# An attention and two-layer MLP kernel: opening in units of 128 queries, with another order of the first weights

## The chip, the cores and the metric

The kernel runs on one core of one Trainium2 chip. The metric is device time in microseconds (us) of one execution. TensorE is called PE, its weight loads PEld, VectorE DVE, ScalarE ACT, GpSimd POOL, SyncE SP.

## What is computed

Attention over chunks of 32 queries, each against 8 memory tokens and its own chunk with 16 tokens to the left and 8 to the right, then two MLPs. There are 4 x 768 = 3072 tokens, 8 heads of 64. The weights and the coefficients a, b arrive as float64; the rest is fp32.

```python
for c in range(nc):                                  # per chunk of 32 queries
    k_full = np.concatenate([mem_k, k[:, :, l_start:r_end]], axis=2)
    v_full = np.concatenate([mem_v, v[:, :, l_start:r_end]], axis=2)
    scores = scale * np.matmul(q_c, k_full.transpose(0, 1, 3, 2))
    a = np.exp(scores - np.max(scores, axis=-1, keepdims=True))
    out[:, :, c_start:c_end] = np.matmul(a / (np.sum(a, axis=-1, keepdims=True) + 1e-09), v_full)
...
h = x @ w_in;   x = np.maximum(0.01 * h, h) @ w_out     # 512 -> 2048 -> 512
...
h = x @ w_in2                                           # 512 -> 2048 -> 512
P = a[0] + a[1]*h + a[2]*h*h + a[3]*h*h*h
Q = 1.0 + np.abs(b[0])*np.abs(h) + np.abs(b[1])*h*h
out = (P / (Q + 1e-06)) @ w_out2
```

## The kernel before

Tokens are worked off in 6 tiles of 512 per layer. Every large matrix product is three products of numbers split in a rounded high part and a low part (high x high, high x low, low x high). A block `emit_h(c)` (L744 on) is 12 products of 128x512 that make 128 hidden features of a tile; `leaky(c)` (L757 on) makes the activation's high part `g` and a copy `s` on ACT and the low part by one subtraction (L766); `emit_y(c)` is the 12 products back to 512 features. There are 16 hidden blocks per tile.

The **opening** (L869 to L950) makes the attention of the first tile. Its 512 queries are 8 blocks of 64, taken two at a time as 4 units. The order of the instructions is written out by hand, and each engine runs its list in that order:

- `att_q` turns a unit's queries on PE (4 transposes, L368) and ACT scales them into `qT` (L370). `att_k` turns one block's keys (L378) and ACT copies them into `kT` or `kT2` (L380); for the first block the memory keys too (L384).
- `att_b1` is one block's scores, 16 products of 64x32 by 64 into a bank `pss` (L460), where four successive products write four different quarters of the array. DVE takes the maximum (L469) and adds its negative (L472), per block on 128x256 numbers. `unit_e` is ACT's exponential of a unit (L412, 128x512); `unit_n` is sum, 1e-9, reciprocal and product (L418 to L421).
- `unit_t` transposes a unit's probabilities (L428), and ACT copies them with four copies of 64x256 (L433) into a block-diagonal tile (`pall`, `pmore`, `pall2`), whose other quarters POOL has set to zero (L876, L877, L881, L882).
- `unit_x` multiplies with the values (16 products of 128x64 by 64 per block pair, L444), ACT rounds to the high part `xh` (L447) and DVE makes the low part `xl` (L448).
- `heat(n)` issues n idle products of 128x128 into a bank `hot` of its own (L867), which nothing reads.

Then comes the **weights' stage** (L978 to L1008): the float64 weights are turned into fp32 in pairs of 128x512 halves, ONE and TWO. `pair_scale` (L170, ACT) scales the high words, `pair_join` is three operations on DVE (L177, L178, L180), `pair_hi` rounds on ACT (L188), `pair_lo` subtracts on DVE (L194). `emit_h(0)`, (1) and (2) are written between them. Pair 0 holds the first layer's input halves 0 and 1, pair 1 input 2 and output 0, pair 2 input 3 and output 1, pair 3 input 4 and output 2, so that `emit_h(4)` needs the high part of pair 3. The order there is

```python
        emit_h(0)
        pair_scale(0, TWO_)
        pair_scale(1, ONE_)
        run(pair_join(0, TWO_))
        pair_hi(0, TWO_)
        run(pair_join(1, ONE_))
        pair_lo(0, TWO_)
        steps = leaky(0)
```

and `steps`, the subtraction of L766, is run later, after the next join. From L1010 a loop goes over all (tile, hidden block) items, with the attention of later tiles put between them by a table of slots. Loads go out on SP's queue in program order: keys and queries, one half of pair 0, values, the other weights.

Of the kernel before, what the change touches and what calls it, by code (L numbers as in the profile page):

```python
# [9 lines left out]
F32 = mybir.dt.float32  # L10
# [14 lines left out]
def kernel(  # L25
# [166 lines left out]
    def pair_lo(n, hs=BOTH):  # L192
        if n < FC:
            nc.vector.tensor_tensor(out=both(n, 1, hs), in0=sums(n, hs).rearrange("p (h m) -> p h m", m=DM),  # L194
                                    in1=both(n, 0, hs).bitcast(F32),
                                    op=ALU.subtract)
# [105 lines left out]
    room = [t[:, n] for t in early for n in range(4)]  # L302
    rooms = {"k": kb + room[0:6], "v": vb + room[6:12], "q": room[12:16]}
# [15 lines left out]
    def load_q(j):  # L319
        bi, blk = divmod(j, BPS)  # L320
        t = rooms["q"][j // 2] if j < FIRST else raw.tile([P, H, D], F32, tag="qr", name="qr", bufs=1)
        nc.sync.dma_start(out=t, in_=q[bi, :, blk * QB:blk * QB + P, :].rearrange("h p d -> p h d"))
        qr[j] = t
# [49 lines left out]
    def att_k(j):  # L373
# [6 lines left out]
        nc.scalar.copy(out=keys(j)[:, :, NM:NM + CTX], in_=pv[:, :, :CTX])  # L380
        if j % BPS == 0:
            for t in (kT, kT2) if j == 0 else (kT,):
                ends = t.rearrange("p c (g m) -> p c g m", m=NM)[:, :, 0:KW // NM:KW // NM - 1, :]
                nc.scalar.copy(out=ends, in_=pv[:, :, KLOAD:].unsqueeze(2).to_broadcast([P, NP, 2, NM]))  # L384
# [6 lines left out]
    opm = {}  # L391
    pall2 = raw.tile([P, 2, NP, 2, 2, CHUNK], F32, tag="wr", name="pb2", bufs=3)
    mall2 = raw.tile([P, 2, NP, WIN], F32, tag="wr", name="pm2", bufs=3)
    kT2 = raw.tile([P, NP, KW], F32, tag="wr", name="kT2", bufs=3)
    pbs = (pall, pmore[:, 0], pmore[:, 1], pall2)

    def keys(j):
        return kT2 if j < FIRST and j % 2 else kT

    def opb(j):  # L400
        return pbs[j // 2]

    def unit_p(j):
        opm[j] = mall2 if j // 2 % 2 else mall
        return opm[j][:, j % 2]

    def span_of(js):
        return slice(js[0] % 2, js[-1] % 2 + 1)

    def unit_e(js):  # L410
        t = opm[js[0]][:, span_of(js)]
        nc.scalar.activation(out=t, in_=t, func=AF.Exp)  # L412

    def unit_n(js):
        t = opm[js[0]][:, span_of(js)].rearrange("p b c m -> p (b c) m")
        n = NP * len(js)
# [6 lines left out]
    def unit_t(js):  # L423
        t = opm[js[0]][:, span_of(js)].rearrange("p b (i h) m -> p (b i) (h m)", h=2)
        n = NP // 2 * len(js)
        ps = psa.tile([P, 512], F32, tag="acc", name="pst")[:, :n * P]
        for i in range(n):
            nc.tensor.transpose(ps[:, i * P:(i + 1) * P], t[:, i, :], ident)  # L428
        pv = ps.rearrange("p (i e c m) -> p i e c m", i=n, e=2, c=2)
        ov = opb(js[0])[:, span_of(js)].rearrange("p b (i h) e c m -> p (b i) h e c m", h=2)  # L430
# [4 lines left out]
    def unit_x(js):  # L435
        n = len(js) * QB
        ps = psa.tile([P, 512], F32, tag="acc", name="psx")[:, :NP * n]
        xv = ps.rearrange("p (c m) -> p c m", c=NP)
        for b, j in enumerate(js):
            vt = rooms["v"][place("v", j)]  # L440
            pt = opb(j)[:, j % 2].rearrange("p n e c m -> p n e (c m)")
            for p in range(NP):
                for e in range(2):
# [425 lines left out]
    with tc.manual_schedule():  # L869
# [15 lines left out]
        for j in range(FIRST):  # L885
            load_qk(j)
# [206 lines left out]
```

## Time and profile before

| | us |
|---|---|
| runs shown | 1149.51, 1150.01, 1151.37 |
| median | 1150.01 |
| profiled execution | 1148.0 |
| its span | 1146.2 |
| PE busy | 1131.7 (99%) |
| DVE busy | 769.7 (67%) |
| ACT busy | 631.8 (55%) |
| POOL busy | 232.1 (20%) |

The span is what the profile covers of the execution; 1.8 us lie around it. A busy share is an average over the span. The profile's first slice of 28.7 us shows PE at 7 tenths, and the slices after it at 9 or more, until the last. Which engine sets the time in a stage is read from the waits there, not from these shares.

### The profile page before, as it was taken

What the parts mean: (1) busy time and instruction counts of PE and PEld (TensorE: products, weight loads), DVE (VectorE), ACT (ScalarE), POOL (GpSimd) and SP (SyncE); (2) the same over time, 40 slices, a digit from 0 to 9 for tenths busy, and PEclk for the clock granted to TensorE, in tenths of its full rate; (3) what the DMA queues carried; (4) which work ended last, traced back from release to release, by engine and by line L of the source; (5) the groups of instructions that cost most, each with busy time, mean ns of one, the idle gap of its engine ahead of it and who ended that gap; (6) DMA issues with size and microseconds to landing.
All of it is one profiled execution on the core that took longest, in us unless ns stands there. A gap on an engine that the chain in (4) does not pass through costs nothing.

```text
span 1146.2 us, 19651 instructions
## 1 busy us (share of the span) xinstructions
PE 1131.7 (99%) x7616; PEld 928.3 (81%) x7616; DVE 769.7 (67%) x1318; ACT 631.8 (55%) x1149; POOL 232.1 (20%) x264
## 2 busy tenths in 40 slices
PE   7999999999999999999999999999999999999998
PEld 6777788888888888888888888888888888888886
DVE  5887846555565555542345886887887888788775
ACT  4677632232232223223346876776777777777765
POOL 3000302231221322210000222222222222222222
PEclk9999999999999999999999999999999999999999
DMA  9966687797778777742342101001100100100101
GB/s 187 260 178 196 187 226 206 213 251 206 202 215 241 208 196 230 207 142 98 97 133 83 65 1 47 28 1 39 36 1 29 46 1 15 59 1 1 37 1 37
DMA packets 148472, 131.98 MB, mean 115 GB/s; under 512 B 63296, under 2 KB 118944, under 8 KB 148380
## 3 DMA queue, kind: packets, MB, share of 16 engines
q1 hardware_dynamic: 143372, 123.25, 37.6%
q0 software_dynamic: 4864, 7.45, 2.8%
q8 instruction: 60, 0.98, 0.4%
q14 instruction: 32, 0.26, 0.1%
q10 hardware_dynamic: 144, 0.03, 0.0%
HBM read 92.92 MB, written 37.75 MB: 114 GB/s over the span
## 4 chain that ended last, share of the span: by engine, by line
PE 95%; DVE 3%; ACT 1%; issue 1%; POOL 0%; DVEq 0%; POOLq 0%
PE hps L753 45%; PE acc L849 23%; PE acc L811 22%; PE psx L667 2%; PE pss L625 1%; PE pss L460 1%; PE hot L867 1%; DVE wwall L178 1%; PE psx L444 0%; PE psx L514 0%; DVE wwall L180 0%; PE psk L378 0%; DVE wwall L177 0%; ACT w L188 0%; DVE w L194 0%
## 5 line engine op out<-in xcount | busy, mean ns | idle before, releaser
L811 PE MATMUL acc<-g,w 128*128 128x512 f32 x1152 | 278.7, 391 | 0.1
L849 PE MATMUL acc<-w,g 128*128 128x512 f32 x1152 | 275.4, 389 | 0.0
L849 PEld LDWEIGHTS acc<-w,g 128*128 128x128 f32 x1152 | 216.2, 188 | 44.8
L811 PEld LDWEIGHTS acc<-g,w 128*128 128x128 f32 x1152 | 214.7, 188 | 46.1 <-ACT w L188 0.5
L763 ACT ACTIVATE g<-hps 128x512 fp32r<-128x512 f32 x96 | 57.4, 598 | 307.1 <-PE hps L753 307.1
L789 POOL TENSOR_TENSOR g<-R,g 128x512 fp32r<-128x512 f32 x96 | 124.2, 1294 | 504.4 <-ACT g L788 466.1
L753 PE MATMUL hps<-xh,w 128*128 128x512 f32 x768 | 209.0, 395 | 3.8 <-ACT pm L484 1.5
L753 PE MATMUL hps<-yh,w 128*128 128x512 f32 x768 | 204.1, 389 | 0.0
L766 DVE TENSOR_TENSOR g<-s,g 128x512 fp32r<-128x512 f32 x96 | 66.2, 690 | 177.6 <-ACT s L764 174.4
L753 PEld LDWEIGHTS hps<-xh,w 128*128 128x128 f32 x768 | 141.2, 188 | 34.6 <-ACT w L188 2.0
L753 PEld LDWEIGHTS hps<-yh,w 128*128 128x128 f32 x768 | 144.3, 188 | 29.9
L590 POOL DMA_DIRECT2D vb<-in_v_dram x128 | 83.2, 651 | 260.5 <-PE psx L667 207.9
L776 ACT ACTIVATE A<-hps 128x512 f32<-128x512 f32 x96 | 57.2, 596 | 113.9 <-PE hps L753 113.9
L792 DVE SCALAR_TENSOR_TENSOR A<-A,small,pb 128x512 f32<-128x512 f32 x96 | 72.0, 750 | 56.2 <-ACT pb L777 56.2
L753 PE MATMUL hps<-xl,w 128*128 128x512 f32 x384 | 103.0, 390 | 0.0
L753 PE MATMUL hps<-yl,w 128*128 128x512 f32 x384 | 102.6, 389 | 0.0
L783 DVE SCALAR_TENSOR_TENSOR A<-A,pb 128x512 f32<-128x512 f32 x96 | 66.5, 692 | 30.2 <-ACT pb L796 30.2
L753 PEld LDWEIGHTS hps<-xl,w 128*128 128x128 f32 x384 | 72.1, 188 | 15.7
L753 PEld LDWEIGHTS hps<-yl,w 128*128 128x128 f32 x384 | 72.1, 188 | 14.9
L778 ACT ACTIVATE R<-hps,small 128x512 f32<-128x512 f32 x96 | 75.0, 781 | 0.0
L785 DVE SCALAR_TENSOR_TENSOR R<-R,small,A 128x512 f32<-128x512 f32 x96 | 72.2, 752 | 3.4
L794 DVE SCALAR_TENSOR_TENSOR R<-R,small,hps 128x512 f32<-128x512 f32 x96 | 71.8, 748 | 3.4
(112 smaller groups left out, 1140.1 us busy)
## 6 DMA issues: line engine op xcount, KB each, us to landing
wr<-in_moe_w_in_dram SPq DMA_DIRECT2D x32, 512.0 KB
wr<-in_moe_w_out_dram SPq DMA_DIRECT2D x32, 512.0 KB
park_dram<-pb SPq DMA_DIRECT2D x16, 512.0 KB
pb<-park_dram SPq DMA_DIRECT2D x64, 128.0 KB
w_dram<-wwall SPq DMA_DIRECT2D x32, 256.0 KB
wb<-w_dram SPq DMA_DIRECT2D x32, 256.0 KB
kb<-in_k_dram SPq DMA_DIRECT2D x59, 112.0 KB
vb<-in_v_dram POOLq DMA_DIRECT2D x118, 56.0 KB, 3.3
```

The source lines that it names most:

```text
L590: nc.gpsimd.dma_start(out=vw[r + at:r + at + n, c], in_=v[bi, hs, lo:lo + n, :].rearrange("h p d -> p h d"))
L753: nc.tensor.matmul(ps[:, :n], w_[:, ws], x_[:, kk, :], start=(kk == 0 and m == 0), stop=(kk == KC - 1 and m == 2))
L763: nc.scalar.activation(out=gh, in_=ps, func=AF.Prelu, alpha=0.01)
L766: return [lambda: nc.vector.tensor_tensor(out=gl, in0=s, in1=gh.bitcast(F32), op=ALU.subtract)]
L778: nc.scalar.activation(out=R, in_=ps, func=AF.Identity, scale=ncf[:, 3:4], bias=ncf[:, 2:3])
L783: nc.vector.scalar_tensor_tensor(out=A0, in0=A0, scalar=ONE, in1=U0, op0=ALU.add, op1=ALU.mult)
L785: nc.vector.scalar_tensor_tensor(out=R0, in0=R0, scalar=ncf[:, 0:1], in1=A0, op0=ALU.add, op1=ALU.mult)
L789: nc.gpsimd.tensor_tensor(out=gl, in0=R0, in1=gh.bitcast(F32), op=ALU.subtract)
L792: nc.vector.scalar_tensor_tensor(out=A, in0=A, scalar=babs[:, 1:2], in1=U, op0=ALU.mult, op1=ALU.add)
L794: nc.vector.scalar_tensor_tensor(out=R, in0=R, scalar=ncf[:, 1:2], in1=ps, op0=ALU.add, op1=ALU.mult)
L811: nc.tensor.matmul(acc[i][d][:, :n], w_[:, ws], g_, start=(f == 0 and m == 0), stop=(f == FC - 1 and m == 2))
L849: nc.tensor.matmul(acc[i][s], g_[:, ss], w_, start=(f == 0 and m == 0), stop=(f == FC - 1 and m == 2))
```

## The change

The opening's unit becomes 128 queries throughout. A unit's scores stand in one bank (`unit_s`, two halves b), with one maximum and one addition of 128x512 (`unit_m`). Its keys come in two pieces (`unit_ka`, 104 or 88 rows; `unit_kb`, 64 rows), and the key tiles are four, two per unit in turn; POOL copies the memory keys into the second two. Successive products of `unit_s` go in pairs to the same quarter of the array. The probabilities are transposed as before but copied with one copy of 128x512; `unit_x` is 32 products of 64x64 by 32 columns into two banks, with two roundings and two low parts of 128x256 per unit. The four POOL memsets go; one of `pall` comes after the opening. The first `heat` has 12 products; idle products write into banks already read. In the weights' stage `pair_lo(0, TWO_)` stands right behind its `pair_hi`, `pair_scale(1, ONE_)` behind that, and four subtractions (the low parts of `leaky(0)`, (1), (2) and of pair 1's second half) are POOL's. The loads go out unit by unit, a unit's queries and then its two key pieces, followed by the values and weights in turn.

```diff
-    def pair_lo(n, hs=BOTH):
+    def pair_lo(n, hs=BOTH, eng=nc.vector):
...
+    kTs = [kT, kT2, kT34[:, 0], kT34[:, 1]]
+    banks = [psw.tile([P, 512], F32, tag="ps", name="hot")]
+    def heat(n, t=None):
+        t = banks[max(len(banks) - 3, 0)] if t is None else t
+        for _ in range(n):
+            nc.tensor.matmul(t[:, :P], ident, ident, start=True, stop=True)
...
+    def unit_ka(u):
+        ps = turned(kroom[u][:, 0], KROWS if u == 0 else CTX, "psk")
+        a, b = kTs[2 * (u % 2)], kTs[2 * (u % 2) + 1]
+        def upper():
+            nc.scalar.copy(out=a[:, :, NM:NM + CTX], in_=ps[:, :, :CTX])
+            if u == 0:
+                for t in (a, b):
+                    nc.scalar.copy(out=ends(t), in_=ps[:, :, KLOAD:].unsqueeze(2).to_broadcast([P, NP, 2, NM]))
+            nc.scalar.copy(out=b[:, :, NM:NM + CTX - KF], in_=ps[:, :, KF:CTX])
...
+    def unit_s(u, b):
+        for p in range(NP):
+            for e in range(2):
+                r = slice(e * 64, e * 64 + 64)
+                for c in range(2):
+                    o = e * 64 + (p % 2) * CHUNK
+                    at = b * QB + c * CHUNK
+                    nc.tensor.matmul(ps[o:o + CHUNK, b, p // 2, c, :], qt[r, p, at:at + CHUNK],
+                                     kt[r, p, c * KOFF:c * KOFF + WIN], start=True, stop=True)
+    def unit_m(u):
+        nc.vector.tensor_reduce(out=mx, in_=ps, op=ALU.max, axis=AX.X, negate=True)
+        nc.vector.tensor_tensor(out=opm[u].rearrange("p (n m) -> p n m", m=WIN), in0=ps,
+                                in1=mx.to_broadcast([P, 2 * NP, WIN]), op=ALU.add)
...
-        for h in range(2):
-            for c in range(2):
-                nc.scalar.copy(out=ov[c * SB:c * SB + SB, :, h, :, c, :], in_=pv[h * SB:h * SB + SB, :, :, c, :])
+        return (lambda: nc.scalar.copy(out=opt[u], in_=ps)), ps
...
+    def unit_x(u, make):
+        for b in range(2):
+            for p in range(NP):
+                for c in range(2):
+                    for e in range(2):
+                        nc.tensor.matmul(ps[c][e * 64:e * 64 + 64, p, b, :], vt[r, 2 * p + e, :],
+                                         pt[r, b, p // 2, e, p % 2, :], start=True, stop=True)
...
-    def leaky(c):
+    def leaky(c, eng=nc.vector):
...
-        heat(6)
+        heat(12)
...
+        for t in (2, 3):
+            nc.gpsimd.tensor_copy(out=ends(kTs[t]), in_=ends(kT))
...
         emit_h(0)
         pair_scale(0, TWO_)
-        pair_scale(1, ONE_)
         run(pair_join(0, TWO_))
         pair_hi(0, TWO_)
+        pair_scale(1, ONE_)
+        pair_lo(0, TWO_)
         run(pair_join(1, ONE_))
-        pair_lo(0, TWO_)
-        steps = leaky(0)
+        run(leaky(0, nc.gpsimd))
         pair_hi(1, ONE_)
         pair_scale(1, TWO_)
         pair_lo(1, ONE_)
         emit_h(1)
         run(pair_join(1, TWO_))
-        run(steps)
-        steps = leaky(1)
         pair_hi(1, TWO_)
         pair_scale(2, ONE_)
-        pair_lo(1, TWO_)
+        pair_lo(1, TWO_, nc.gpsimd)
+        run(leaky(1, nc.gpsimd))
         emit_h(2)
         run(pair_join(2, ONE_))
-        run(steps)
-        steps = leaky(2)
+        run(leaky(2, nc.gpsimd))
```

**First place: DVE, two units of the opening.** `mx` is the maximum, `pm` (and `pm_105`, `pm_104`, `pb`) the tile of probabilities, `sm` the sums. Before:

```order
L469 TENSOR_REDUCE mx<-pss 128x4
L472 TENSOR_TENSOR pm_105<-pss,mx 128x256
L469 TENSOR_REDUCE mx<-pss 128x4
L472 TENSOR_TENSOR pm_105<-pss,mx 128x256
L418 TENSOR_REDUCE sm<-pm 128x8
L419 TENSOR_SCALAR sm<-sm 128x8
L420 RECIPROCAL sm<-sm 128x8
L421 TENSOR_TENSOR pm<-pm,sm 128x512
L469 TENSOR_REDUCE mx<-pss 128x4
L472 TENSOR_TENSOR pm<-pss,mx 128x256
L469 TENSOR_REDUCE mx<-pss 128x4
L472 TENSOR_TENSOR pm<-pss,mx 128x256
```

and now, from the first unit on:

```order
L472 TENSOR_REDUCE mx<-pss 128x8
L473 TENSOR_TENSOR pm<-pss,mx 128x512
L483 TENSOR_REDUCE sm<-pm 128x8
L484 TENSOR_SCALAR sm<-sm 128x8
L485 RECIPROCAL sm<-sm 128x8
L486 TENSOR_TENSOR pm<-pm,sm 128x512
L472 TENSOR_REDUCE mx<-pss 128x8
L473 TENSOR_TENSOR pm_104<-pss,mx 128x512
```

Two maxima and two additions of a unit have become one of each, over twice the columns, and the first unit's sums now stand ahead of the second unit's maximum.

**Second place: PE, from one unit's keys to the next.** `psk` and `psq` are turned keys and queries, `pss` scores, `pst` turned probabilities, `hot` the idle products. Before:

```order
L867 MATMUL hot<-ident 128x128 x2
L368 MATMUL psq<-ident,early 128x128 x4
L378 MATMUL psk<-ident,early 128x88 x8
L867 MATMUL hot<-ident 128x128
L428 MATMUL pst<-ident,pm 128x128 x4
L460 MATMUL pss<-kT,qT 32x64 x16
L460 MATMUL pss<-kT_106,qT 32x64 x16
```

and now:

```order
L427 MATMUL psk<-ident,early 128x64 x4
L463 MATMUL pss<-kT,qT 32x64 x16
L407 MATMUL psq<-ident 128x128 x2
L427 MATMUL psq<-ident,early 128x128 x4
L427 MATMUL psk<-ident,early 128x64 x4
L427 MATMUL psk<-ident,early 128x88 x4
L463 MATMUL pss<-kT_105,qT 32x64 x16
L407 MATMUL psq<-ident 128x128 x2
L491 MATMUL pst<-ident,pm 128x128 x4
L463 MATMUL pss<-kT_106,qT 32x64 x32
```

The transposes of a unit's probabilities stood between the next unit's keys and scores; they now stand behind the scores of two further units.

**Third place: DVE in the weights' stage,** from the second half of pair 0 on. `wwall` is the joined weights (three operations per half), `w` the low part (L194), `g` the activation's low part. Before:

```order
L177 TENSOR_SCALAR wwall<-wwall 128x512
L178 SCALAR_TENSOR_TENSOR wwall<-wr_93,wwall 128x512
L180 SCALAR_TENSOR_TENSOR wwall<-wr_93,wwall 128x512
L194 TENSOR_TENSOR w<-wwall,w 128x512 x2
L177 TENSOR_SCALAR wwall<-wwall 128x512
L178 SCALAR_TENSOR_TENSOR wwall<-wr_93,wwall 128x512
L180 SCALAR_TENSOR_TENSOR wwall<-wr_93,wwall 128x512
L766 TENSOR_TENSOR g<-s,g 128x512
L194 TENSOR_TENSOR w<-wwall,w 128x512
```

now:

```order
L194 TENSOR_TENSOR w<-wwall,w 128x512
L177 TENSOR_SCALAR wwall<-wwall 128x512
L178 SCALAR_TENSOR_TENSOR wwall<-wr_93,wwall 128x512
L180 SCALAR_TENSOR_TENSOR wwall<-wr_93,wwall 128x512
L194 TENSOR_TENSOR w<-wwall,w 128x512
L177 TENSOR_SCALAR wwall<-wwall 128x512
L178 SCALAR_TENSOR_TENSOR wwall<-wr_93,wwall 128x512
L180 SCALAR_TENSOR_TENSOR wwall<-wr_93,wwall 128x512
L177 TENSOR_SCALAR wwall<-wwall 128x512
```

and on POOL, around the end of the opening:

```order
L345 COPY early<-early 32x1536
L1046 MEMSET pb 128x1024
L829 TENSOR_TENSOR g<-s,g 128x512
L194 TENSOR_TENSOR w<-wwall,w 128x512
L829 TENSOR_TENSOR g<-s,g 128x512 x2
L652 DMA vb<-in_mem_v_dram 8x4x64
```

On DVE the low part of each half now comes right behind its join, with no subtraction of `g` between; on POOL four subtractions stand behind the memset of `pall` and ahead of the later tiles' loads.

## Rows read from the trace of the kernel before

**Rows 1.** Page, part 4: the chain that ended last, by engine.
```profile
PE 95%; DVE 3%; ACT 1%; issue 1%; POOL 0%; DVEq 0%; POOLq 0%
```

**Rows 2.** Windows: from:to us, length, busy us (x) of PE, PEld, DVE, ACT, POOL, PEclk, DMA, GB/s.
```profile
0.00:34.49 34.49, 27.45 (x512) 24.18 (x512) 19.50 (x48) 18.51 (x43) 11.32 (x16) 1.00 1.02 219
34.49:54.29 19.80, 18.28 (x80) 14.07 (x81) 17.45 (x28) 12.27 (x21) 0.00 (x0) 1.00 0.87 225
54.29:84.00 29.71, 29.70 (x284) 23.30 (x284) 25.85 (x39) 22.60 (x62) 0.00 (x0) 1.00 0.65 191
```

**Rows 3.** Chain in order of time, start of the weights' stage and its end: start, us, what.
```profile
35.04 0.44 DVE wwall L177
...
53.19 1.05 ACT w L188
54.29 1.88 PE hps L753 x7
```

**Rows 4.** Timeline of the opening: start us, us, engine, line, tiles, count, [idle before].
```profile
1.37 2.93 PE L867 MATMUL hot<-ident 128*128 128x128 f32 x12 [1.37 <-POOL ident masks.py:199]
4.09 1.06 PE L368 MATMUL psq<-ident,early 128*128 128x128 f32 x4
6.24 0.45 ACT L380 COPY kT<-psk 128x352 f32<-128x352 f32 x1 [0.46 <-PE psk L378]
7.03 0.71 PE L460 MATMUL pss<-kT,qT 64*32 64x64 f32 x32
8.20 0.43 DVE L469 TENSOR_REDUCE mx<-pss 128x4 f32<-128x256 f32 x1
8.30 0.64 PE L867 MATMUL hot<-ident 128*128 128x128 f32 x4
```

**Rows 5.** Timeline, one unit in the steady part of the opening.
```profile
16.79 1.50 ACT L433 COPY pb<-pst 64x256 f32<-64x256 f32 x4 [0.99 <-PE pst L428]
17.81 0.42 DVE L472 TENSOR_TENSOR pm<-pss,mx 128x256 f32<-128x256 f32 x1
18.15 0.41 DVE L469 TENSOR_REDUCE mx<-pss 128x4 f32<-128x256 f32 x1
18.94 0.68 DVE L418 TENSOR_REDUCE sm<-pm 128x8 f32<-128x512 f32 x1
20.01 0.65 ACT L412 ACTIVATE pm<-pm 128x512 f32<-128x512 f32 x1
20.09 0.69 DVE L421 TENSOR_TENSOR pm<-pm,sm 128x512 f32<-128x512 f32 x1
```

**Rows 6.** Window on DVE's work from its first maximum to its last low part.
```profile
8.20:34.89 26.69, 21.14 (x456) 18.52 (x455) 18.20 (x41) 16.34 (x38) 4.08 (x4) 1.00 1.08 239
```

**Rows 7.** Timeline, one cycle of the weights' stage on DVE.
```profile
40.00 0.42 DVE L177 TENSOR_SCALAR wwall<-wwall 128x512 uint32<-128x512 uint32 x1
41.80 0.68 DVE L766 TENSOR_TENSOR g<-s,g 128x512 fp32r<-128x512 f32 x1
41.92 0.62 ACT L188 CAST w<-wwall 128x512 fp32r<-128x512 f32 x1
42.57 0.69 DVE L194 TENSOR_TENSOR w<-wwall,w 128x512 fp32r<-128x512 f32 x1
43.18 0.42 DVE L177 TENSOR_SCALAR wwall<-wwall 128x512 uint32<-128x512 uint32 x1
```

**Rows 8.** Groups by form, 34 to 54 us: busy, mean ns | idle before.
```profile
L170 ACT ACTIVATE wwall<-wr 128x512 f32<-128x512 f32 x5 | 3.3, 671 | 0.0
```

**Rows 9.** Timeline around a subtraction on POOL in the second layer, DVE and POOL.
```profile
698.56 1.29 POOL L789 TENSOR_TENSOR g<-R,g 128x512 fp32r<-128x512 f32 x1 [4.15 <-ACT g L788]
698.68 0.75 DVE L794 SCALAR_TENSOR_TENSOR R<-R,small,hps 128x512 f32<-128x512 f32 x1
699.85 0.69 DVE L783 SCALAR_TENSOR_TENSOR A<-A,pb 128x512 f32<-128x512 f32 x1 [0.42 <-ACT pb L796]
```

**Rows 10.** Groups by form, 0 to 35 us: score products and their weight loads.
```profile
L460 PEld LDWEIGHTS pss<-kT,qT 64*32 64x32 f32 x256 | 3.9, 108 | 0.9 <-issue 0.3 <-ACT kT L380 0.3 <-ACT kT L384 0.2
```

More of the change, by code (lines that the diff above doesn't have):

```diff
@@ L301 @@
     FIRST = tiles_of[0][0][1] // QB
-    room = [t[:, n] for t in early for n in range(4)]
-    rooms = {"k": kb + room[0:6], "v": vb + room[6:12], "q": room[12:16]}
+    rooms = {"k": kb, "v": vb + [early[1][:, n] for n in (2, 3)] + [early[2][:, n] for n in range(4)]}
     def place(kind, j):
@@ L407, in span_of @@
[L407 to L416, printed above, removed]
+    kT34 = raw.tile([P, 2, NP, KW], F32, tag="wr", name="kT34", bufs=3)
+    kroom = [kall[:, 0:2], early[0][:, 0:2], early[0][:, 2:4], early[1][:, 0:2]]
+    kTs = [kT, kT2, kT34[:, 0], kT34[:, 1]]
@@ new lines, with bank @@
+    half = lambda t, n: t.rearrange("p a b c d e -> p (a b c d e)")[:, n * 512:(n + 1) * 512]
+    opm = [mall.rearrange("p b c m -> p (b c m)"), mall2.rearrange("p b c m -> p (b c m)"),
+           half(pall, 0), half(pall, 1)]
+    opt = [pmore.rearrange("p n a b c d e -> p (n a b c d e)")[:, u * 512:(u + 1) * 512] for u in range(4)]
+    oqT, ops = {}, {}
+    banks = [psw.tile([P, 512], F32, tag="ps", name="hot")]
+    def bank(name):
+        banks.append(psw.tile([P, 512], F32, tag="ps", name=name))
+        return banks[-1]
@@ new lines, in turned, with unit_q @@
+    def turned(t, rows, name):
+        ps = bank(name)[:, :NP * rows].rearrange("p (c m) -> p c m", c=NP)
+        t = t.rearrange("p h d -> p (h d)")
+        for p in range(NP):
+            nc.tensor.transpose(ps[:, p], t[:rows, p * P:(p + 1) * P], ident[:rows, :rows])
+        return ps
+    def unit_q(u):
+        ps = turned(early[3][:, u], P, "psq")
+        o = tmp.tile([P, NP, P], F32, tag="A", name="qT")
+        oqT[u] = o
+        return lambda: nc.scalar.mul(out=o, in_=ps, mul=scale)
@@ L861, with run @@
     ONE_, TWO_ = slice(0, 1), slice(1, 2)
-    hot = psa.tile([P, 512], F32, tag="acc", name="hot")
-    def heat(n):
-        for _ in range(n):
-            nc.tensor.matmul(hot[:, :P], ident, ident, start=True, stop=True)
+    def run(fns):
+        for fn in fns:
+            fn()
     with tc.manual_schedule():
@@ L919 @@
-        heat(2)
-        unit_e(unit[U - 1])
-        unit_t(unit[U - 2])
-        pair_scale(0, ONE_)
-        lower.append(unit_x(unit[0]))
-        heat(2)
-        unit_n(unit[U - 1])
-        unit_t(unit[U - 1])
-        lower.append(unit_x(unit[1]))
-        lower.pop(0)()
-        for fn in pair_join(0, ONE_):
-            fn()
+        unit_s(0, 0)
+        heat(2)
+        up_a1 = unit_ka(1)
+        up_a1()
+        up_q1 = unit_q(1)
+        up_q1()
+        unit_s(0, 1)
+        heat(2)
@@ new lines @@
+        unit_m(0)
+        up_b1 = unit_kb(1)
+        up_b1()
+        unit_e(0)
+        unit_n(0)
+        unit_s(1, 0)
+        heat(2)
+        up_q2 = unit_q(2)
+        up_q2()
+        up_a2 = unit_ka(2)
+        up_a2()
+        unit_s(1, 1)
+        heat(2)
+        unit_m(1)
+        up_b2 = unit_kb(2)
+        up_b2()
+        unit_e(1)
+        unit_n(1)
+        unit_s(2, 0)
+        heat(2)
+        up_q3 = unit_q(3)
+        up_q3()
+        up_b3 = unit_kb(3)
+        up_b3()
+        up_a3 = unit_ka(3)
@@ new lines @@
+        up_a3()
+        unit_s(2, 1)
+        heat(2)
+        unit_m(2)
+        up_t0, spare = unit_t(0)
+        up_t0()
+        unit_e(2)
+        unit_s(3, 0)
+        unit_s(3, 1)
+        heat(2)
+        unit_m(3)
+        up_t1, _ = unit_t(1)
+        up_t1()
+        unit_e(3)
+        unit_n(2)
+        x0 = unit_x(0, bank)
+        x0[0]()
+        heat(2)
+        pair_scale(0, ONE_)
+        x1 = unit_x(1, bank)
+        x1[0]()
+        heat(2, spare)
+        unit_n(3)
+        up_t2, _ = unit_t(2)
@@ L1003 @@
         run(pair_join(2, TWO_))
-        run(steps)
         pair_hi(2, TWO_)
```

184 lines of the change are left out of this document (90 added, 94 removed).

## The prediction

> **What bounds the kernel now.** I read the chain that ended last, then the busy time by stage, then the chain and the timeline of the two stages that the change touches. The chain is 95% PE and 3% DVE [rows 1], so a gain must come from the few stretches where PE isn't the end of it. The windows show where they are [rows 2]: until 34.49 us PE is busy 27.45 of 34.49; in the weights' stage, 34.49 to 54.29, 18.28 of 19.80; from 54.29 on 29.70 of 29.71. So 54.29, the start of `emit_h(4)`, is the point to follow: behind it PE has no gap that could absorb a shift, and a shift of that point goes to the end unless a later stage takes it back. Ahead of it two chains follow one another. In the opening it goes through PE, ACT and DVE a unit at a time. In the weights' stage it is DVE's from 35.04 on, until ACT rounds pair 3 at 53.19 (1.05) and `emit_h(4)` starts [rows 3].
>
> The profiled execution took 1148.0 (span 1146.2 and 1.8 around it), 2.0 under the median of the runs shown, 1150.01. The shifts below are worked out in that execution and subtracted from the median.
>
> **The first scores come later.** Six idle products are 12 records and took 2.93, 0.24 a record; later the same ones take 0.64 for 4, 0.16 each [rows 4], though the PEclk column reads 1.00 for the whole opening [rows 2], which is its 2.4 GHz level. The first `heat` now has 12 products, so 12 records more: +2.9 at the early price, +1.9 at the later one. I take +2.9, since they stand in the same early stretch, and keep the difference of 1.0 for the range. So the queries' transposes start near 1.37 + 2 x 2.93 = 7.2 instead of 4.09. From there to the first scores it took 2.94 (4.09 to 7.03); with transposes at about 0.6 instead of 1.06, and the keys' too, I take 1.9, so the first half's scores start at 9.1 and not 7.03. The maximum used to wait for one half and now waits for both, and on PE two idle products, the next unit's turned keys and turned queries stand between the halves: about 0.5 + 0.4 + 0.5 + 0.6 + 0.5 + 0.2 for DVE's memset, so the first maximum is at 11.9, where it was at 8.20 [rows 4]. That is **+3.7**.
>
> **DVE's opening gets shorter.** From its first maximum to its last low part DVE had 18.20 of work in 26.69 [rows 6]; 8.5 were waits, most of them for the next unit's scores, which stood behind the transposes of the unit before last. Now DVE's list holds, for each of 4 units, a maximum and an addition of 128x512, priced as the sum's row (0.68) and the product's (0.69): 1.4; sum to product again 1.84 (18.94 to 20.78) [rows 5]; one join 1.8 and one low part 0.7, as in the weights' stage [rows 7]; eight low parts of 128x256, at the 0.34 to 0.42 of operations of that width that read PSUM (17.81 to 18.15) [rows 5], 0.37 each. Together 5.5 + 7.4 + 2.5 + 3.0 = 18.4. The scores now come ahead of DVE's need, because the transposes are out of their way, so what is left as waits is the exponential (0.65 [rows 5]) ahead of the sums of the first two units, with handovers 1.4. The last low part ends near 11.9 + 18.4 + 1.4 = 31.7 instead of 34.89: **-3.2**. `emit_h(0)` needs the high parts first and moves with it, to about 31.2.
>
> **What costs nothing here.** Four copies (1.50 a unit [rows 5]) become one, off the path: DVE has other units' work meanwhile. POOL's memsets are waited for by nobody. The value products double in number, on a PE that idles 7 of 34.49 [rows 2]; were the last unit's on the path, it would be some tenths more. The loads are no larger, and the weights' scaling on ACT never waited for one (idle 0.0 [rows 8]). With everything 3.2 earlier the loads come nearer: what is left of that cover I don't know, and at worst it costs as much as the 3.2, the lower end of the gain. Outside of that the SP queue's order puts each weight at its old place behind the values.
>
> **The weights' stage gets longer.** Four subtractions of 0.69 leave DVE, but little of this is gain. Before, the cycle of a half was 3.18 (40.00 to 43.18): join 1.8, the subtraction of `g` at 41.80, low part at 42.57; and the rounding on ACT that the low part waits for ran beside it, 41.92 to 42.54 [rows 7]. Now the low part stands right behind its join, and DVE waits for the rounding: 1.87 + 0.65 + 0.61 (42.57 to 43.18) = 3.13, practically the same. Before, the stage had 18.2 of DVE from 34.89 to 53.13. Now: 5 joins x 1.87 = 9.3, four low parts x 0.61 = 2.4, four waits for a rounding x 0.65 = 2.6, the last join of 128x1024 at 3.2 (49.95 to 53.19 less its handover [rows 3] bounds it). To this comes a new wait: the scaling of pair 2's first half (0.67 [rows 8]) stands on ACT behind the rounding of pair 1's second half (0.62), which waits for the join before; DVE used to do `g` and a low part meanwhile, and now has only the next join: 1.3. The other scalings are met by 0.1 to 0.5, 0.7 in all. Sum 19.5, so the stage is **+1.3** longer, and all four subtractions on POOL come to no one's harm if POOL runs beside DVE: 1.29 each [rows 9], where `emit_y(0)` alone may wait some tenths.
>
> **The sum**: -3.2 + 1.3 = -1.9 at `emit_h(4)`, 52.4 instead of 54.29. 1150.01 - 1.9 = **1148.1**. This case's own ends: with the idle products at 0.16, 1.0 less; with the scores' halves close together 0.8 less; with last products and handovers on the path 1.4 more: 1146.3 to 1149.5. A measurement of this kernel can tell 0.2%, 2.3 us: 1147.7 to 1152.3 counts as no change.
>
> **Rivals.** *The opening does better.* DVE's 1.4 of waits go because the sums find their exponential done, and half of the added idle products (1.2) is at the later price: 1148.1 - 2.6 = 1145.5. For it: the idle products halve in price within the opening [rows 4]. Against: nothing in DVE's list stands between a unit's addition and its own sums for the first two units.
>
> *POOL and DVE get in each other's way.* In the weights' stage DVE's joins and low parts read two tiles in SBUF each, and so do POOL's subtractions. Where POOL subtracts in the second layer, the operation beside it (698.68) has an operand in PSUM, and the next one with both in SBUF starts at 699.85, exactly when POOL's ends [rows 9]; but the row gives ACT as what it waited for, so it can't tell. If such a pair can't overlap, POOL's 1.29 goes into DVE's chain where it comes first: most of two of them in front of a join (1.2 + 1.2), the rest behind it (0.3 + 0.4), +3.0: **1151.1**, slower than before; it decides from the moment at which two of the four start ahead of DVE's join. If the joins' first operation, with one tile, waits too, +4.2: 1152.3.
>
> The Trainium skill, "SBUF — State Buffer", section "Who interferes with whom", says that a DVE instruction with two SBUF inputs and a GpSimd instruction that reads SBUF exclude each other for their whole length, in order of issue. It speaks for this rival against my forecast; the trace of before agrees with it and does not show it.
>
> *The score products get slow.* Pairs of successive products now use the same quarter of the array. A weight load takes 0.108 [rows 10]; if half of each pair's second one shows, a half has 8 x 0.05 = 0.4 more, and with two to all eight halves on DVE's path the end moves by +0.8 to +3.2: 1148.9 to 1151.3. Against: a product is recorded twice already, on the same quarter both times. The Trainium skill, "TensorE: Matmul & The Clock Gate", section "What overlaps and what doesn't", says that a weight load runs beside a product in flight only where their row groups differ; no row here shows it for such a pair.
>
> *The change does nothing at the end*, because a load that was hidden comes last: 1150.0; it is in the no-change part of the cases above.
>
> **How the numbers follow.** Forecast 0.42 (its range lies across the bound: 0.19 faster, 0.23 the same), the better opening 0.19 (faster), POOL against DVE 0.25 (0.13 the same, 0.12 slower with its upper price and the forecast's upper end), slow score products 0.14 (0.06 and 0.08, when added to POOL's). Faster 0.38, same 0.42, slower 0.20. The range reaches from 1145.2, just past the better opening, to 1152.8, past POOL's upper price; what is outside is a tenth on either side.
>
> **What would show it.** First maximum at 11.9; last low part of the opening at 31.7; DVE with hardly a wait longer than 0.7 in between; in the weights' stage a wait of 0.6 ahead of each low part and one of 1.3 ahead of pair 2's first join; `emit_h(4)` at 52.4. Wrong would be: operations of DVE with two SBUF tiles that last well over 0.69 or start at the end of a POOL subtraction; score halves of 0.9; an idle time of ACT's scaling that a load ends; or a shift at 52.4 that is not there at the end.

## The result, and the profile after

The changed kernel takes 1156.62 us in the median (1155.04 to 1157.76, 4 runs) against 1149.76 of the kernel before on the same chip: ratio 1.0056, interval 1.0039 to 1.0074. It is slower by 6.9, where the forecast was 1.9 faster. Its profiled execution took 1156.17, 8.2 more than that of before. Three executions in the study, one each in e2, e5 and e8, ran at a far lower clock and are left out of all figures below; e5's profile was one of them, so no row of e5 is shown.

The windows of the changed kernel by stage, columns as in [rows 2]:

```profile
0.00:37.25 37.25, 29.82 (x641) 26.79 (x641) 18.45 (x41) 15.63 (x38) 9.07 (x15) 0.91 1.01 221
37.25:61.74 24.49, 21.40 (x81) 16.40 (x81) 18.52 (x25) 12.10 (x21) 5.56 (x4) 0.86 0.58 142
61.74:91.45 29.71, 29.71 (x284) 23.29 (x284) 25.79 (x39) 22.66 (x62) 0.00 (x0) 1.00 0.65 193
```

`emit_h(0)` starts at 37.25 where it was at 34.49, and `emit_h(4)` at 61.74 where it was at 54.29: +2.8 from the opening, +4.7 from the weights' stage. From there PE is full again, as before [rows 2], and the shift of 7.45 stays; the profiled pair loses some tenths more in small waits behind 143 us, which were not followed up. PEclk, the granted clock of PE as a share of its 2.4 GHz, is new: 0.91 and 0.86 where it was 1.00.

The timeline of the changed kernel (start us, us, engine, line; in brackets the idle time before and what ended it):

```profile
8.36 0.69 PE L463 MATMUL pss<-kT,qT 64*32 64x64 f32 x32
11.30 0.69 DVE L472 TENSOR_REDUCE mx<-pss 128x8 f32<-128x512 f32 x1
25.70 0.66 PE L507 MATMUL psx<-pmore,early 64*64 64x32 f32 x29 [1.13 <-issue]
30.32 1.41 DVE L517 TENSOR_TENSOR xl<-psx,xh 128x256 fp32r<-128x256 f32 x4
35.20 1.49 PE L507 MATMUL psx<-pmore,early 64*64 64x32 f32 x43 [4.38 <-issue]
36.95 0.76 DVE L517 TENSOR_TENSOR xl<-psx,xh 128x256 fp32r<-128x256 f32 x2 [5.22 <-ACT xh L513]
```

The first maximum comes near its forecast (11.9), and at 31.7, where the last low part was forecast, three of the four units have theirs. But PE stops twice in the value products, for 1.13 and, in the middle of the last unit, for 4.38; the last low part ends at 37.71, not at 31.7. "Issue" means that PE waited for nothing that the profile shows. These lengths are idle time. Counted from the start of the last record ahead of them the stops are 1.35 (24.35 to 25.70) and 4.60 (30.60 to 35.20). The windows around the two, PE alone (length, busy, count, PEclk, DMA share, GB/s):

```profile
24.00:26.00 2.00, 0.87 (x56) 1.00 0.56 118
26.00:28.00 2.00, 2.00 (x34) 0.76 0.96 204
30.00:32.00 2.00, 0.82 (x38) 0.89 1.06 376
32.00:34.00 2.00, 0.00 (x0) 0.96 1.08 389
34.00:36.00 2.00, 0.80 (x32) 0.50 1.05 374
38.00:40.00 2.00, 2.00 (x7) 0.50 1.14 213
```

Behind the first stop and during the second the granted clock falls to its lower level of 1.2 GHz (0.50), the second time through most of `emit_h(0)`. It is not what makes PE stop: the column reads 1.00 from 24 to 26, when the first stop begins. From 30 to 36 us the loads run at 374 to 389 GB/s. In the DMA view of the two us in which PE does nothing, from 32 to 34, one row is of another kind, a queue that carries instructions (packets, MB, share):

```profile
q8 instruction: 1, 0.02, 3.3%
```

In the weights' stage DVE and POOL read:

```profile
43.53 1.36 DVE L194 TENSOR_TENSOR w<-wwall,w 128x512 fp32r<-128x512 f32 x1 [0.69 <-ACT w L188]
47.92 1.04 DVE L177 TENSOR_SCALAR wwall<-wwall 128x512 uint32<-128x512 uint32 x1 [1.25 <-ACT wwall L170]
48.94 2.99 POOL L829 TENSOR_TENSOR g<-s,g 128x512 fp32r<-128x512 f32 x2 [0.26 <-DMA small<-in_moe_a_dram]
49.00 1.79 DVE L178 SCALAR_TENSOR_TENSOR wwall<-wr,wwall 128x512 uint32<-128x512 uint32 x1
50.83 1.65 DVE L180 SCALAR_TENSOR_TENSOR wwall<-wr,wwall 128x512 uint32<-128x512 uint32 x1
```

Before, L177 took 0.42 and L194 0.69 [rows 7], and L178, like L180, 0.69 (groups by form, 34 to 54 us):

```profile
L178 DVE SCALAR_TENSOR_TENSOR wwall<-wr,wwall 128x512 uint32<-128x512 uint32 x5 | 3.5, 692 | 0.2
```

Now one of each takes 1.36 (L194), 1.04 (L177), 1.79 (L178) and 1.65 (L180), together 3.35 more, and POOL's two last subtractions take 2.99 where one took 1.29 [rows 9].

### The profile page after: what moved, and what is told of

The parts are those of the page before. It is cut to its first block, busy times and chain, and to the rows that moved or that the text cites. A ratio compares the mean times of both kernels' runs of the same rounds, so it can differ in the third digit from the quotient of the medians.

```text
span 1154.4 us, 19892 instructions
## 1 busy us (share of the span) xinstructions
PE 1137.8 (99%) x7744; PEld 932.9 (81%) x7744; DVE 769.2 (67%) x1308; ACT 629.1 (54%) x1144; POOL 236.4 (20%) x267
## 3 DMA queue, kind: packets, MB, share of 16 engines
q0 software_dynamic: 4864, 7.45, 2.7%
## 4 chain that ended last, share of the span: by engine, by line
PE 92%; SPq 3%; DMA 2%; DVE 1%; ACT 1%; issue 1%; DVEq 0%
PE hps L816 44%; PE acc L912 23%; PE acc L874 22%; PE psx L730 2%; PE pss L688 1%; SPq L315 1%; SPq L166 1%; DMA kb<-in_k_dram 1%; DMA early<-in_k_dram 1%; DVE wwall L178 0%; PE pss L530 0%; PE psx L577 0%; DMA pb<-park_dram 0%; DVE wwall L180 0%; ACT wwall L170 0%
```

## The experiments

Two theories stand. **Instructions**: PE stops because its instructions arrive in pieces of 256, and the opening uses them up faster than they come. **Exclusion**: DVE and POOL can't work at the same time on operands in SBUF. The rivals are a late load of values or the granted clock for the stops, and the waits for roundings for the stage's length.

| run | kernel | median | before, same chip | ratio (95%) |
|---|---|---|---|---|
| e1 | change, subtractions on DVE | 1153.42 | 1148.91 | 1.0027 (1.0011 to 1.0044) |
| e2 | change, weights' stage of before | 1153.98 | 1148.91 | 1.0038 (1.0025 to 1.0051) |
| e3 | change, weights held by 2 us | 1156.90 | 1148.91 | 1.0059 (1.0039 to 1.0080) |
| e4 | change, 6 idle products first | 1155.98 | 1148.91 | 1.0060 (1.0045 to 1.0075) |
| e5 | before, new weights' stage | 1153.66 | 1148.92 | 1.0042 (1.0025 to 1.0059) |
| e6 | change, weights held longer | 1153.42 | 1148.92 | 1.0038 (1.0023 to 1.0053) |
| e7 | e6, weights' stage of before | 1150.09 | 1148.92 | 1.0007 (0.9998 to 1.0017) |
| e8 | e7, 6 idle products first | 1150.58 | 1148.92 | 1.0013 (1.0003 to 1.0023) |
| e9 | e8, no idle products later | 1146.46 | 1149.02 | 0.9981 (0.9972 to 0.9991) |
| e10 | e7, twice the later idle products | 1151.14 | 1149.02 | 1.0015 (1.0006 to 1.0024) |
| e11 | before, new order, all on DVE | 1152.17 | 1149.02 | 1.0029 (1.0018 to 1.0040) |
| e12 | before, four subtractions on POOL | 1152.09 | 1149.02 | 1.0031 (1.0019 to 1.0043) |
| e13 | e2, idle products as in e9 | 1145.80 | 1148.47 | 0.9977 (0.9968 to 0.9987) |

### Where PE stops: e4

```diff
-        heat(12)
+        heat(6)
```

> The changed kernel with 6 idle products at the start instead of 12, so 24 PE instructions fewer ahead of everything. Theory 'instructions come in pieces of 256': both gaps stand again at the 961st and the 1217th of PE's records, that is 12 products' records later in the program (near the 47th of unit 1's 64 value products' records and the 33rd of unit 3's, where they were the 35th and the 21st). Rival 'a semaphore, the values or a bank': the gaps stay at the 35th and the 21st. Time within 1.5 of 1156.6 by the first, since the transfer decides when the gap ends; by the second up to 2 less, as the first scores come 2.7 earlier.

The windows of PE and PEld that end in each stop, first of the changed kernel, then of e4 (busy us and, in brackets, count):

```profile
0.00:24.50 24.50, 23.13 (x471) 20.79 (x472) 12.28 (x27) 11.30 (x28) 8.12 (x14) 1.00 1.02 174
0.00:32.00 32.00, 28.33 (x597) 25.43 (x597) 18.15 (x40) 14.93 (x35) 9.07 (x15) 0.95 1.01 195
```

```profile
0.00:24.80 24.80, 22.91 (x471) 19.85 (x472) 12.66 (x27) 12.06 (x28) 8.12 (x14) 1.00 0.98 182
0.00:31.00 31.00, 26.59 (x597) 23.15 (x597) 18.24 (x40) 14.95 (x35) 9.08 (x15) 1.00 0.97 199
```

Both kernels stop after 471 and after 597 product records, though e4 has 6 products (12 records) fewer ahead. Counted with weight loads and semaphore instructions, as the trace has them, these are the 961st and the 1217th record of PE. So the place in the program moved, and the timeline of e4 shows by how much (and a short stop ahead, which the changed kernel doesn't have):

```profile
15.92 0.42 PE L463 MATMUL pss<-kT,qT 64*32 64x64 f32 x9 [0.52 <-issue]
...
23.80 1.01 PE L507 MATMUL psx<-pmore,early 64*64 64x32 f32 x47
25.50 0.44 PE L507 MATMUL psx<-pmore,early 64*64 64x32 f32 x17 [0.69 <-issue]
...
27.74 1.71 PE L507 MATMUL psx<-pmore,early 64*64 64x32 f32 x97 [0.28 <-issue]
34.14 1.07 PE L507 MATMUL psx<-pmore,early 64*64 64x32 f32 x31 [4.69 <-issue]
```

Unit 1's value products break off after 47 records (35 in the changed kernel), and the 97 behind 27.74 are unit 2's 64 and 33 of unit 3 (21 before): exactly the 12 records of the expectation. A semaphore on a load or a bank belongs to an instruction and would have stopped the same one. Between the two stops lie 126 products and 125 weight loads, and with the five semaphore instructions of PE in the trace 256 instructions. The short stop of e4, at 15.92, stands 512 of PE's instructions ahead of the first of the two. For the first stop the profile names a load of values as well (1.2 on PEld); e4 shows that it wasn't the load. Nor was it the clock: in e4 it reads 1.00 up to 31.00, and the second stop begins at 29.45. The time moved little, as expected.

The instruction queue says what ends a stop. In the changed kernel its transfers run from 22.80 to 24.16 and from 32.76 to 33.81, and PE goes on at 25.70 and 35.20. So it is at every stop of every kernel here: PE goes on 1.2 to 1.6 after a transfer of that queue has ended. The queue's 61 transfers in the changed kernel, at 256 instructions each, also fit PE's program: 7744 product records, as many weight loads and 223 semaphore instructions. Pace alone doesn't make a stop. From the 449th record to the 705th PE took 4.8 and did not stop, and the next piece had been sent for 1.6 after the 449th. Up to the first stop it took 3.7, and the piece was sent for 2.2 after the 705th; up to the second it took 4.9, and the piece was sent for 7.1 after the 962nd, with which PE had gone on.

### What makes the piece late: e3, e6, e7, e10

e3 holds the weights from pair 1 on behind a one-column memset on DVE (after the first join); e6 and e7 load the second half of pair 0 first and hold the rest until the low part of pair 0's first half; e7 has the weights' stage of before as well. The edit of e6 and e7 in the loads:

```diff
+        pair_load(0, TWO_)
         for j in range(4, FIRST):
             load_v(j)
-        pair_load(0, TWO_)
-        pair_load(1)
...
         pair_lo(0, ONE_)
+        nc.vector.memset(raw_half(1, 0)[:, 0:1], 0)
+        pair_load(1)
```

> The changed kernel with the loads of the weights from pair 1 on held back until the first join is done (a one-column memset of their tile, some 2 us later than now). Theory 'PE waits for its own instructions, whose transfer stands behind the weights': the instruction transfer that came at 32.8 comes before 30, the gap of 4.4 goes, emit_h(0) starts near 33 instead of 37.2, about 1152.5. Rival 'the last values land late for want of descriptors, not of bandwidth': the gap stays above 3, time within 1 of 1156.6.

> The changed kernel with the second half of pair 0 loaded ahead of the last values and all further weights held until the low part of pair 0's first half is done (near 30). Theory 'the transfer of PE's instructions stands behind the weights' transfers': the instruction transfer at 32.8 comes before 29.5, the gap of 4.4 shrinks under 1, emit_h(0) starts near 33 and the time falls by 3 to 5, to about 1152.5. Rival 'that transfer is asked for late, whatever else is moving': it still comes 6 to 7 after the crossing (25.7), the gap stays above 3.

> As e6_hold_more, with the weights' stage in the order of the kernel before, all subtractions on DVE: the opening's gain without the gap and without POOL. If both theories hold: emit_h(0) near 32.5, the stage 19.4 to 20, emit_h(4) near 52.5, some 2 us faster than the kernel before, about 1147.5. If the gap stays: as e2_tail_before, +5 over before.

e3 gained nothing: in its trace the instruction transfer came at 32.6 and the second stop was 3.7. e6 and e7 did empty the queues: the +6.9 of the changed kernel became +4.5 in e6 (their intervals overlap a little), and the +5.1 of e2 became +1.2 in e7, a drop clear of the noise, though not to the 1147.5 that was expected. e7 at its second stop, in windows and timeline:

```profile
28.00:30.00 2.00, 2.00 (x26) 1.67 (x26) 0.38 (x2) 0.94 (x2) 0.18 (x1) 0.50 0.00 1
30.00:32.00 2.00, 1.27 (x78) 1.16 (x73) 1.22 (x4) 1.40 (x4) 0.77 (x1) 0.96 0.03 8
```

```profile
26.10 0.66 PE L507 MATMUL psx<-pmore,early 64*64 64x32 f32 x29 [1.67 <-issue]
...
32.83 0.91 PE L507 MATMUL psx<-pmore,early 64*64 64x32 f32 x43 [1.56 <-issue]
```

The second stop shrank from 4.38 to 1.56. But with 1 GB/s moving between 28 and 30 the transfer still came only at 30.4, more than 4 us after PE had gone on at 26.10. So the weights make the second stop longer, by some 3, and are not its root; both the theory of e6 and its rival held in part. Why the next piece comes so late after this stop even with idle queues is open.

e10 is e7 with more idle products, at ten places:

```diff
-        heat(2)
+        heat(4)
```

> As e7_hold_more_tail_before, with 4 idle products in place of 2 at each later place: 80 PE instructions more. Theory of the instructions: gaps at the 961st and 1217th record again, each as long or longer, and one more boundary (1473) close behind; time 0.5 to 2 over e7 (1150.1). Rival 'gaps come from the clock or from idle PE': more idle products close them, and the time is equal or lower.

```profile
28.54 1.25 PE L507 MATMUL psx<-pmore,early 64*64 64x32 f32 x64 [0.57 <-ACT wwall L170]
...
32.04 2.18 PE L507 MATMUL psx<-pmore,early 64*64 64x32 f32 x128 [0.28 <-issue]
```

What the theory expected of the gaps fell, and what the rival expected of them came: the stop behind the 961st record shrank to 0.57 (1.67 in e7; the row names a wait for ACT, but PE goes on 1.5 after an instruction transfer here too), the one behind the 1217th had gone, and the clock stayed at 1.00. The 256 instructions up to the 961st record now took 4.3 instead of 3.8, and the next piece was sent for 1.2 after PE went on, not 4.3 after; why so early is open. But the rival's reason, the clock, doesn't hold, by e4. And the time didn't fall: `emit_h(0)` came no earlier (34.87, and 34.37 in e7), and `emit_h(4)` at 56.03 against 56.41; the median's rise of 1 comes later, as 1.4 between 136 and 164 us in the trace, and was not followed up. The stops were 2.7 shorter; the 20 more idle products are work for PE too (where 4 records took 0.71, 8 take 1.16, at ten places), and presumably took that back. So a full clock that is bought with idle products gained nothing.

### Fewer instructions: e8, e9, e13

> As e7_hold_more_tail_before with 6 idle products at the start. If the first scores set the opening's end (the prediction's +3.7): up to 2.5 faster than e7, about 1145. If the later pace is set by DVE, loads or PE's instructions: the same as e7 within 0.7.

e8 is within 0.7 of e7: its first maximum is earlier (10.37 against 11.15 in the traces), but its stop behind the 961st record is 2.61, and that takes the gain back. So the first idle products are not what the opening waits for.

> As e7_hold_more_tail_before, with 6 idle products at the start and none later: 104 PE instructions fewer in the opening. Theory 'PE runs out of instructions because the opening has too many per us': the crossings at the 705th and 961st record come later, the gap at the 961st (1.9 in e7) is under 0.5 and the next one under 1; emit_h(0) near 32, about 1147.5 if the clock stays at 1.00. Rival 'the idle products hold the clock': the granted clock falls to 0.5 before 24 us, where it was 1.00 in e7, and the time is 1150 or more.

> As e2_tail_before (loads in the order of the change, weights' stage of the kernel before) with the idle products of e9_lean: 6 at the start and none later. If too many PE instructions per us make the gap and the weights' transfers only lengthen it: the gap at the 961st record stays under 1, the one at the 1217th under 2, and the time is within 1.5 of e9 (1146.5). If the weights' transfers make it: a gap of 3 or more comes back, and the time is near e2's 1154.

```diff
-        heat(12)
+        heat(6)
...
-        heat(2)
```

(the last at all ten places). In e9 and e13 both that is the edit, and both are faster than the kernel before. e13, without the hold, is at 0.9977 (0.9968 to 0.9987); it can't be told from e9 (0.9981), so the hold isn't needed. e13 differs from e2 (1.0038) by 26 idle products alone, which are 104 PE instructions. Its timeline (DVE, then PE) and clock:

```profile
11.07 0.69 DVE L472 TENSOR_REDUCE mx<-pss 128x8 f32<-128x512 f32 x1
...
28.17 1.41 DVE L517 TENSOR_TENSOR xl<-psx,xh 128x256 fp32r<-128x256 f32 x4
30.34 0.76 DVE L517 TENSOR_TENSOR xl<-psx,xh 128x256 fp32r<-128x256 f32 x2 [0.75 <-ACT xh L513]
```

```profile
23.48 1.08 PE L491 MATMUL pst<-ident,pb 128*128 128x128 f32 x4 [0.32 <-DVE pb L486]
25.24 1.09 PE L491 MATMUL pst<-ident,pb 128*128 128x128 f32 x4 [0.68 <-DVE pb L486]
26.26 3.65 PE L507 MATMUL psx<-pmore,early 64*64 64x32 f32 x128
30.63 2.07 PE L816 MATMUL hps<-xh,w 128*128 128x512 f32 x4 [0.72 <-ACT xh L513]
```

```profile
24.00:26.00 2.00, 1.32 (x7) 0.50 0.58 122
28.00:30.00 2.00, 1.91 (x72) 0.50 1.05 325
```

PE now waits for DVE's probabilities ahead of both transposes, and the 128 records of value products behind them run without a stop, since the boundary at the 961st record now falls behind that wait. One stop is left behind the 705th record, 0.64 long (up to 21.34 in the trace); DVE has work through it and waits for nobody. The last low part ends at 31.10, `emit_h(0)` is at 30.63 and `emit_h(4)` at 51.64. And this with the clock at 0.50 from 24 to 32: the full clock is not needed for the gain.

Two things are not separated here. The idle products that went were instructions and also time on PE: the stops are 5.6 shorter than in e2 in all, and the last low part comes 7.7 earlier (31.10 against 38.80). And where the boundaries fall in the program is luck: none of the kernels chose it.

### The weights' stage: e1, e2, e5, e11, e12

e12 changes in the kernel before only the engine of the four subtractions, e11 only the order (the diff of the weights' stage above, without its `nc.gpsimd`), e5 both. e12:

```diff
-        steps = leaky(0)
+        steps = leaky(0, nc.gpsimd)
...
-        pair_lo(1, TWO_)
+        pair_lo(1, TWO_, nc.gpsimd)
```

> The kernel before in its own order, with only the engine of the four subtractions changed to POOL. Theory 'POOL and DVE exclude each other': DVE's joins that run beside one last 1.0 to 1.8 instead of 0.42 and 0.69, and the time is +2 to +4. Rival 'they run beside each other': durations as before, each half's cycle 3.17 as before since the rounding is waited for instead, time within 1 of before.

> The kernel before with the weights' stage in the order of the change, but all four subtractions on DVE. By the prediction's price of the order (waits for roundings and scalings 4.6, less what the subtractions fill): 0 to +1.3 over before. Together with e5_before_new_tail (+4.8) it tells what POOL alone costs; if POOL and DVE exclude each other, at least 3 of those 4.8 are gone here.

> The kernel before with only the weights' stage of the change (its order, and the four subtractions on POOL); the opening is the old one, so no gap of PE's instructions stands ahead. Theory 'POOL and DVE exclude each other': operations of DVE with two tiles last over 1.3 where a POOL subtraction runs, and the stage from 34.89 to 54.29 (19.4) becomes 2.7 to 4 longer: about 1152. The prediction's own price of the order without any collision: 1.3 longer, about 1150.

The engine alone costs 3.1, with the kernel before around it. e12's groups by form on DVE, 35 to 58 us, where before each of the first three took 0.69 and L177 0.42:

```profile
L178 DVE SCALAR_TENSOR_TENSOR wwall<-wr,wwall 128x512 uint32<-128x512 uint32 x5 | 4.4, 888 | 0.2
L180 DVE SCALAR_TENSOR_TENSOR wwall<-wr,wwall 128x512 uint32<-128x512 uint32 x5 | 4.4, 884 | 0.2
L194 DVE TENSOR_TENSOR w<-wwall,w 128x512 fp32r<-128x512 f32 x4 | 3.7, 924 | 1.5 <-ACT w L188 1.4
L177 DVE TENSOR_SCALAR wwall<-wwall 128x512 uint32<-128x512 uint32 x5 | 2.7, 545 | 1.4 <-ACT wwall L170 1.2
```

In e1, with the subtractions on DVE, the same lines read again

```profile
L178 DVE SCALAR_TENSOR_TENSOR wwall<-wr,wwall 128x512 uint32<-128x512 uint32 x5 | 3.5, 691 | 0.2
L177 DVE TENSOR_SCALAR wwall<-wwall 128x512 uint32<-128x512 uint32 x5 | 2.1, 423 | 0.1
```

so the lengthening is the collision. The Trainium skill, "SBUF — State Buffer", section "Who interferes with whom", says that a DVE instruction with two SBUF inputs contends with a GpSimd instruction that reads SBUF. The trace agrees: two of DVE's operations beside POOL's pair took 1.79 and 1.65, each about 1 more than 0.69, and POOL's pair itself 2.99 instead of 2 x 1.29 [rows 9]. One waiting for the whole of the other, as the theory has it, is not quite what it shows: both sides got longer, and the four operations together lasted 3.54 (48.94 to 52.48), where one after another they would have taken 3.96. The first operation of the join, with one tile, is hit too (1.04 in the changed kernel).

The order alone costs 3.2 (e11), more than forecast. Its timeline on DVE has

```profile
38.44 0.69 DVE L194 TENSOR_TENSOR w<-wwall,w 128x512 fp32r<-128x512 f32 x1 [0.69 <-ACT w L188]
44.77 0.69 DVE L194 TENSOR_TENSOR w<-wwall,w 128x512 fp32r<-128x512 f32 x1 [0.69 <-ACT w L188]
46.32 0.69 DVE L765 TENSOR_TENSOR g<-s,g 128x512 fp32r<-128x512 f32 x1 [0.85 <-ACT s L763]
```

three waits of 0.69 for a rounding (the third at 52.65) and one of 0.85 for the activation `s`, which the new order wants right away where the old one ran a join first. Together they are 2.9, and by 2.9 the stage from the last low part to `emit_h(4)` grew in its profile (22.3, from 19.4). e5 has order and engine, +4.7, a little over what was expected and less than the sum of the two, 6.2. The two don't add up, since e11 keeps the subtractions on DVE and e5 doesn't; over e12, which has them on POOL as e5 does, the order costs 1.7.

e1 undoes the engine in the changed kernel, and e2 all of the weights' stage, back to the order of the kernel before:

```diff
-        run(leaky(0, nc.gpsimd))
+        run(leaky(0))
...
-        pair_lo(1, TWO_, nc.gpsimd)
+        pair_lo(1, TWO_)
```

> The changed kernel with its four subtractions back on DVE, the order otherwise as changed. Theory 'POOL and DVE exclude each other': DVE's operations between 43 and 53 us, which last 1.04, 1.36, 1.65 and 1.79, last 0.42 to 0.69 again, and the stretch from the opening's last low part (37.71) to emit_h(4) (61.74), 24.0 now, shrinks by 3 to 4; about 1153. Rival 'the waits for the rounding make the stage long': the durations fall but the stretch stays within 1 of 24.0, since DVE has four subtractions more; about 1156.

> The changed kernel with the whole weights' stage in the order of the kernel before. If only the engine of the subtractions matters, this equals e1_subs_on_dve within 1 us (about 1153). If the order of joins and low parts matters as the prediction priced it (1.3), it is about 1 us faster than that. The gap of 4.4 in the last unit's value products (30.8 to 35.2) stays in both.

Both have lower medians than the changed kernel (+4.5 and +5.1 against +6.9; the intervals overlap a little) and are still slower than the one before: the stops are in both, 4.2 and 4.7 of idle time for the second. From the end of the opening's last low part to `emit_h(4)` the profiles give 24.0 in the changed kernel, 22.7 in e1, 20.5 in e2 and 19.4 before, so the 3 to 4 expected of e1 in the profile were 1.4 for the engine and 2.2 more for the order. The medians of e1 and e2 don't show that order (their intervals overlap; e1's runs lie from 1147.61 to 1155.18), so what the order costs inside the changed kernel is taken from the profile alone.

The 1.1 by which the stage of e2 is longer than before, in the same order, goes with the lower clock: with PEclk at 0.50, `emit_h(1)` comes 4.26 after `emit_h(0)` where it came 3.14 after, ACT's activation waits 1.38 for PE, and DVE for the rounding behind that. No run takes the clock alone away. e13's stage is as long (20.5) by another wait, that of ACT's scaling for a load, of which 0.83 reaches DVE. First e2, then e13:

```profile
44.42 0.69 DVE L194 TENSOR_TENSOR w<-wwall,w 128x512 fp32r<-128x512 f32 x1 [1.26 <-ACT w L188]
```

```profile
33.40 0.68 ACT L170 ACTIVATE wwall<-wr 128x512 f32<-128x512 f32 x1 [2.03 <-DMA wr<-in_moe_w_in_dram]
```

## Why the prediction was wrong

**What bounds the kernel** was right: the shift at `emit_h(4)` is the shift at the end, +7.45 and a median of +6.9.

**The first scores**: 11.30 against 11.9, right in size. The cause was half wrong. The six added idle products were priced at 2.9; in e4, without them, the first maximum is at 10.41, 0.9 earlier, and in e13 it is still at 11.07. There PE waits for the load of the second unit's keys, which now stand on PE ahead of the first unit's second half:

```profile
8.88 0.49 PE L427 MATMUL psk<-ident,early 88*128 88x88 f32 x4 [1.46 <-DMA early<-in_k_dram]
```

A profile can't tell less than about 1 here: the changed kernel, e1 and e2 have the same opening, and their first maxima are at 11.30, 10.48 and 11.63.

**DVE's opening gets shorter**: right as a sum, 31.7 forecast for the last low part, 31.10 in e13, where no stop reaches DVE. In the changed kernel it was 37.71.

**The step that failed first** is the one under "What costs nothing here": the doubled value products on a PE with idle time were priced at some tenths. Their cost isn't PE time. They and the idle products brought PE past 256 instructions in 3.7 (from 20.6 to 24.35) and again in 4.9, which is faster than the pieces came, and PE stopped for 1.35 and 4.60 (with the last record ahead of each). e4 shows that the boundary stops PE, and in e13, with one short stop left, the delay is gone. Together they are 6.0, as much as the distance from 31.7 to 37.71. That it fits so well is in part luck: DVE still had work through the first stop, and the lower clock stretched PE's work between the two (85 value product records took 2.35, where 64 at full clock took 1.14). Before, 256 instructions took 5.4 and more there, and none was missed.

**The step that failed second** is the sentence on POOL in "The weights' stage gets longer", that its subtractions come to no one's harm. The rival, at +3.0 with chance 0.25, was the truth: +3.1 in e12. Its upper price, with the one-tile operation, has its row too. (The rival's four parts add up to 3.1, not 3.0, which changes nothing.)

**The price of the order**, +1.3, was right for the kernel that was changed. Its waits are there: 0.68 or 0.69 ahead of each of the four low parts (0.65 in the sum) and 1.25 ahead of pair 2's first join (1.3). With the 3.35 by which the four operations beside POOL got longer they make 4.65, and the stage grew by 4.7. The 3.2 of e11 is another price: there the subtractions are on DVE, and one of them waits 0.85 for ACT's `s`.

**The score products** were no slower: a half took 0.71 [rows 4] and takes 0.69 on pairs of the same quarter. The rule on weight loads weighed there (the Trainium skill, "TensorE: Matmul & The Clock Gate", section "What overlaps and what doesn't") goes by row groups, and can't tell the two kernels apart: in both, the two products of a pair take the same 64 rows, and only the columns changed. So no run here tests it. **A late load** was not the cause of the stops, but the weights' loads lengthened the second, and the sign that was named, ACT's scaling waiting for a load, is there in e13 (2.03).

The range ended at 1152.8 because no case had the opening late by something outside the engines' work, and the only two rivals that it added up were the slow score products and POOL's. Here two steps failed at once: 6.0 in the opening and 3.4 in the weights' stage.

## What to carry to other kernels

Count instructions as well as time: where a stretch of one engine's program runs several hundred short instructions close together, its supply of instructions can set the pace. Idle products spend from the same supply; they take time as well, so more of them can also close a stop, without a gain (e10). A subtraction is not free on POOL when DVE works on SBUF tiles beside it; try the engine change alone before building an order on it. Where an engine's work in a wait is moved away, ask what covers that wait next. The kernel to keep is e13: the new opening with 6 idle products at its start and none between, and the old weights' stage.

## What the runs showed of the hardware that was not expected

- PE's program is supplied in pieces of 256 instructions, 0.02 MB each in the profile's instruction queue. The Trainium skill, "Runtime: NRT & Kernel Launch", section "Instruction fetch mechanics", gives the same size and calls the cost mostly hidden; here it showed as stops of 1.13 and 4.38.
- PE went on 1.2 to 1.6 after an instruction transfer had ended, at every stop of every kernel here.
- After a stop the next transfer started as little as 1.2 (e10) and as much as 8.1 (e1) after PE went on, and 4.3 after with 1 GB/s on the queues (e7); what it waits for is open.
- A 128x512 operation of DVE with two SBUF tiles took 1.36 to 1.79 beside a subtraction of POOL, 0.69 alone; a pair on POOL took 2.99 beside DVE, and 1.29 is the time of one alone.
- The granted clock fell to its lower level behind the stop of 1.13 and during that of 4.38 in the changed kernel, and in e13 by 24 us, behind a stop of 0.64 and a wait of 0.32 ahead of a transpose; e10, with more idle products, kept it at 1.00 and has the ratio 1.0015 where e13 has 0.9977.
